# One fixed issue order replaced by another in a fused long-convolution and local-attention kernel

## The chip, the cores and the metric

The kernel runs on one core of one Trainium2 chip, as one program in one launch. The metric is the device time of that core in microseconds (us). The kernel before takes 234.37 us, the median of three runs (234.35 to 235.52).

The core has a matmul engine (PE, whose weight loads the profile lists apart as PEld), a vector engine (DVE), an activation engine (ACT), a general engine (POOL) and a queue engine (SP). Each works through its own instruction list in order, and an instruction that waits holds up all that stand behind it in its list. Matmul results land in PSUM and are copied from there by ACT or DVE.

## The reference

x is A_q, of 2048 rows (positions) and 640 columns, in bfloat16. Two branches read it, and a gate for each row mixes them.

```
g = sigmoid((x * gate_w).sum(-1))
# A: a causal convolution as long as the sequence
k_shift = 4-tap causal filter of A_k along the positions
kv = k_shift * A_v
y  = irfft(rfft(kv, 2S) * rfft(ssm_k, 2S))[:S] + kv * ssm_D
a  = x * y
# B: attention of 32 heads of 20 columns; position s sees s, s-2, ..., s-14
q, k, v = split(x @ wqkv)
b = softmax(q . k / sqrt(20), over the 8 positions) . v  @ wo
out = g * a + (1 - g) * b
```

## The kernel before, in words

**Attention.** x is transposed by PE (`xpose`, L449) into xT. `vproj` (L525) makes v, and `qkproj` (L572) makes q and k transposed, for five column blocks ft, into staging tiles stg. `fragger` (L619 to L622) then moves the rows of each head by DMA from stg to 32-row slots in three sets of tiles, qb and kb, most of them issued from POOL's queue. `score_gen` multiplies qb by kb for four heads at a time (L648), ACT takes the exponential into ETall (L655), `pv_gen` multiplies by v (L679), and DVE divides by the sums (L689, L692). `op_tr` transposes the result, and `outproj` (L879) multiplies it by wo in 32 units of five matmuls. Each unit is copied out by ACT (L884) or DVE (L886) into bl, scaled by 1 - g.

**Convolution.** DVE filters A_k in eight blocks of seven instructions (`conv`, L471 to L486) and multiplies by v (L490). The transform of the 2048 positions is done in two matmul stages, for the filter (`h_stream`) and the data (`u_stream`), each for two halves P of the columns: `s1_unit` (L713, L715) and `s2_unit` (L734). Each unit is copied out of PSUM by ACT (L244) or DVE (L246). The filter's transform is kept twice: in place (H for half 0, SX for half 1) and with its two partition halves swapped (Hw). The swap (`swaps`, L830) goes in four steps of two DMAs per half; between two steps POOL copies one element (L824), so that a step waits until the one before it has landed. `products` (L766) multiplies both forms by the data's transform on DVE, 22 instructions per half. `inverse1` (L845) is the first inverse stage, ten units of 16 matmuls per half, and `final` (L927) the second, in six pieces of two or three groups of rows.

**The end.** `load_q` brings x in again, 1024 rows at a time: q0 for pieces 1 to 3 of `final`, q1 for pieces 4 to 6. Each of the two is four DMAs on SP's queue (L902). The third and fourth are paced: POOL reads one element of the first (second) part out of q into link (L897), so it waits for that part's landing, and clears one element of the next part (L898), which the next DMA waits for. DVE then scales q by g in eight instructions (L905). For each piece, DVE multiplies the piece by q (L939), adds bl (L941), and four DMAs on SP's queue write it out (L944). They wait for L941.

**What sets the order.** The parts are generators that yield requests (an engine or a choice of two, dependencies, PSUM slots). `Steps.run` reads the string ORDER: each letter names a generator, whose pending request is granted and its instructions issued; a `-` ahead of it picks the second of two engines (DVE for a copy out of PSUM). The string therefore fixes each engine's list, the engine of each copy and, because slots are handed out first in, first out, the PSUM slot of each unit. There are four slots of two banks; a small unit takes half of one. Costs, moves and lags that stand in the requests are read by nothing in this program. Waits are put in by the framework wherever one instruction needs another's data or tile. The DMAs of `final` are no requests: they are issued in the same step as L941.

Of the kernel before, what the change touches and what calls it, by code (L numbers as in the profile page):

```python
# [17 lines left out]
S = 2048  # L18
D = 640
# [94 lines left out]

STREAMS = "abcdefghijklmnopqrstuvwxyz0123456789ABCDEFGHIJKLMNOPQRSTUVWXYZ"
ORDER = """
a-aa-aw-wawww-aiw-ia-awwi-ii-iaaiia-aa-aaaw-wi-ii-ii-iifiiiiii-iiifwwcccwwwwcfcccccccccccfffwwwwcwfwwwffccwww-ww-wcccccccccwwwffww
wfdddddccccciccccccccccccccccxff-xfifcidiifficcccfiiddddddccixxiccxciiffdxddefiidfiifeicccccccii-iiiiidddxxxxxffxxxffdfffcccfxxxxx
-xxxi-idddddexedddddii-xfiiiiiiffdddffxlccccxieidddfedcdiii-iddddfiiiy-iyy-yyxiyyxiyy-yyiyx-idddddecfcd-xxed-xccccdccfcccccccccccc
icccciiifdddyiyiecdfffdddediifidiccdcdddifeddcc-iccdfdie-iid-idddfdi-iifyi-yyyyyeiidedidddddx-ixfx-xdyyy-yccccccccy-yyjiyjccccccci  # L120
fccdddddidedddjff-iif-idyj-ydicccccdidddeedddiifefgiidcddddiii-icdeccccdccccgcdjjdddie-ididd-iiiiiddcdgcccclgcccedddeyyycc-yyyycdd
-yccyyy-yccjddeedzddd-zdcccdzc-zzzz-zoddzdd-zzzz-zeddddeddzd-zzdddd-zzoodd-zdeeddddz-zzzz-zddzzzdqde-zdddddozoooooeduzz-zzzoeezzz
-zzz1-111111-1111-1111-111000-0001-1ooo00uu0-000oooooo000-00-00ooo0r0-r10-101r021rr2221-r1r-r00221111r-ru111111ss3ss1313111331ss3u
s333s3333333333p333ss00220020ss0ss2ssss000s002s0000555555555550552252222uvv225vv55522254-5-44-4vvvv4444u4vv-444u444vvvu444puuuuu4
-4tts-stvtststtsssssst-tts-ss-ssss-ssttstttsss-ss-stssttstt-tsts-sttttttsstsstssssttts-ssttst
"""


# [88 lines left out]
def kernel(  # L217
# [21 lines left out]
    def raw(ap, off, dims):  # L239
        return bass.AP(tensor=ap.tensor, offset=ap.offset + off, ap=dims)  # L240
# [27 lines left out]
    G = p0.tile([128, 32, 2, 128], BF, name="G", tag="G")  # L268
# [40 lines left out]
    def ev(name):  # L309
        if name not in E:  # L310
            E[name] = Ev()
        return E[name]

    def mark(name, g, lag=0.0):
        x = ev(name)
        x.src, x.lag = g.done.src, lag
# [48 lines left out]
    def bulk(ft):  # L365
        if ft == 0:
            yield from load_k(1)
            yield from load_k(2)
            g = yield Req("G", 3900.0)
            masks(2)  # L370
            yield from load_corners()
            yield from small()
            yield from load_h(0)
        if ft == 1:
            for a in range(4):
                yield from load_G(a)
                yield from load_v(0, a)
        if ft == 2:
            for a in range(4):
                yield from load_v(1, a)  # L380
        if ft == 3:
            yield from load_h(1)
# [213 lines left out]
    def fragger():  # L596
        left = {}
        for h in range(H):
            for f in range(DH * h // 128, (DH * h + DH - 1) // 128 + 1):
                left[h // 4] = left.get(h // 4, 0) + 2  # L600
        for ft in range(NDT):
            f0 = 128 * ft
            hs = list(range(f0 // DH, (f0 + 127) // DH + 1))
            got = {}
            for h, w in ([(h, w) for h in hs for w in range(2)] if ft == 0 else [(h, w) for w in range(2) for h in hs]):
                if w not in got:
                    yield Req("N", 0.0, [ev(f"pj{ft}{w}")])
                    got[w] = frags.pop(0)
                    assert got[w][:2] == (ft, w)
                _, _, stg, evs, free = got[w]  # L610
                wd = KW if w else QW
                fa, fb = max(DH * h, f0), min(DH * h + DH, f0 + 128)
                t, rows = h // 4, fb - fa
                r0 = 32 * (h % 4) + fa - DH * h
                dst = (ksets if w else qsets)[t % 3]
                deps = list(evs) + ([ev(f"sc{t - 3}")] if t >= 3 else [])
                near = ft == 0 and w == 0
                if near:
                    g = yield Req("S", 450.0, deps, move=20.0 * rows)  # L619
                else:  # L620
                    g = yield Req("G", 510.0, deps, move=20.0 * rows)
                (nc.sync if near else nc.gpsimd).dma_start(dst[r0:r0 + rows, 0:wd], stg[fa - f0:fb - f0, 0:wd])  # L622
                left[t] -= 1
                if near:
                    mark(f"near{t}", g)
                if not left[t]:
                    mark(f"set{t}", g)
                if h == hs[-1]:
                    free.src = g.done.src
            yield from bulk(ft)  # L630
        mark("frags", g)
# [258 lines left out]
    def load_q(half):  # L890
        yield Req("N", 0.0, [ev(f"{k}s2{P}") for k in "hu" for P in range(2)] if half else [ev("hs10"), ev("hs11")])
        q = p0.tile([128, 8, D], BF, name=f"q{half}", tag="G" if half else "HL")
        st[f"q{half}"] = q
        for g in range(4):
            if g > 1:
                x = yield Req("G", 200.0, [r0.done])
                nc.gpsimd.tensor_copy(link[32 * g - 64:32 * g - 32], q[32 * g - 64:32 * g - 32, 0, 0:1])  # L897
                nc.gpsimd.memset(q[32 * g:32 * g + 32, 0, 0:1], 0.0)  # L898
            if g:
                r0 = r  # L900
            r = yield Req("S", 600.0, [x.done] if g > 1 else [], move=1450.0)
            nc.sync.dma_start(q[32 * g:32 * g + 32], raw(x2, (32 * (g // 2) + g % 2 + 16 * half) * D, [[64 * D, 32], [2 * D, 8], [1, D]]))  # L902
        for t in range(8):
            r = yield Req("D", 297.0, [Ev(r.done.src, 2500.0), ev("gate")] if t == 0 else [])
            nc.vector.tensor_scalar(q[:, t], q[:, t], g_nat[:, 8 * half + t:8 * half + t + 1], None, ALU.mult)  # L905
        mark(f"qg{half}", r)

# [40 lines left out]
    for gen in (xpose, h0_slot, fragger, score_gen, pv_gen, conv, conv_v, conv_end, qkproj, gate, x_slot, h_slot, p2_slot,  # L948
                u_slot, swaps, load_T, load_wo, op_tr, outproj, final):
        plan.add(gen(), gen.__name__)  # L950
    for gen in (load_q, vproj, h_stream, u_stream, products, inverse1):
        for P in range(2):
            plan.add(gen(P), f"{gen.__name__}{P}")
# [31 lines left out]
```

## Time and profile before

| | |
|---|---|
| three runs | 234.35, 234.37, 235.52 us |
| the profiled execution, a fourth | 235.92 us, with a span of 233.9 us from first to last instruction |
| granted PE clock over the span | 0.966 of full |
| matmuls / weight loads / DVE / ACT / POOL instructions | 3537 / 3537 / 272 / 250 / 137 |
| moved by DMA | 33.86 MB, mean 145 GB/s |

Busy time is what the profile counts while an engine runs an instruction. A queue name with a q behind it (SPq, POOLq) is the engine's sequencer, which waits for semaphores and issues DMAs. In a timeline row stand the start, the length, the engine and line, the operation with tiles and shapes, and in brackets the idle time before it with what ended it. In a row of stretches stand, for each engine, the busy time and the number of instructions, then the granted PE clock as a share of full speed.

### The profile page before, as it was taken

How to read it: one execution, taken by the hardware profiler on the slowest of the kernel's cores; microseconds unless marked ns; L12 is line 12 of the kernel's file. 1: busy time of each engine (PE TensorE's matmuls, PEld its weight loads, DVE VectorE, ACT ScalarE, POOL GpSimd, SP SyncE). 2: the span in 40 equal slices, each digit the busy share in tenths (PEclk: the TensorE clock that was granted, in tenths of full speed). 3: DMA queues.
4: the chain of work that ended last, by engine and by line, in shares of the span. 5: the costliest groups of instructions: out<-in, count | busy, mean ns of one | idle time of the engine just before them, and what ended most of it. 6: DMA issues, size and time to landing. Idle time of an engine off the chain costs nothing.

```text
span 233.9 us, 8338 instructions
## 1 busy us (share of the span) xinstructions
PE 213.4 (91%) x3537; PEld 172.5 (74%) x3537; DVE 190.7 (82%) x272; ACT 173.0 (74%) x250; POOL 60.1 (26%) x137
## 2 busy tenths in 40 slices
PE   7999999788999999999998898999999599889890
PEld 3886987567767767767676587988887499889770
DVE  4655997995877898789999877999659996967971
ACT  0343659436989999898999878997999396765480
POOL 6900780443061622712350000000000390000000
PEclk9999999979999999999999859999999799999998
DMA  6999599699999999879747675474590509003545
GB/s 208 354 196 295 145 184 173 130 137 141 177 186 197 199 151 152 147 125 123 114 98 195 172 169 116 109 175 115 119 196 7 112 3 205 3 3 87 124 116 131
DMA packets 69560, 33.86 MB, mean 145 GB/s; under 512 B 51476, under 2 KB 67220, under 8 KB 69524
## 3 DMA queue, kind: packets, MB, share of 16 engines
q1 hardware_dynamic: 66356, 28.35, 62.7%
q0 software_dynamic: 2880, 4.90, 9.8%
q8 instruction: 27, 0.44, 0.8%
q10 hardware_dynamic: 288, 0.09, 0.2%
q14 instruction: 9, 0.07, 0.1%
HBM read 20.04 MB, written 2.62 MB: 97 GB/s over the span
## 4 chain that ended last, share of the span: by engine, by line
PE 52%; DVE 17%; DMA 14%; issue 6%; POOL 4%; ACT 3%; SPq 1%; DVEq 0%; POOLq 0%
PE PS L572 15%; PE PS L879 6%; DMA Hw<-SX 6%; PE PS L679 5%; PE PS L845 5%; PE PS L648 5%; DVE SX L246 4%; PE PS L525 4%; PE PS L734 3%; DMA kb<-stg 3%; DVE SX L766 3%; DVE Hw L766 3%; DMA q<-in_A_q_dram 2%; PE PS L927 2%; DMA KX<-in_A_k_dram 2%
## 5 line engine op out<-in xcount | busy, mean ns | idle before, releaser
L655 ACT ACTIVATE ETall<-PS 121x912 bf16<-121x912 f32 (+1 forms) x80 | 64.7, 867 | 6.5 <-PE PS L648 6.2
L572 PE MATMUL PS<-xT,Wqk 128*128 128x342 bf16 (+1 forms) x300 | 50.5, 313 | 2.3 <-DVE VW L692 2.0
L244 ACT CAST UC<-PS 128x1024 bf16<-128x1024 f32 (+2 forms) x47 | 43.6, 1053 | 8.4 <-PE PS L845 4.9
L572 PEld LDWEIGHTS <-Wqk 128*128 128x128 bf16 x300 | 27.8, 98 | 17.3 <-issue 2.9
L471 DVE TENSOR_TENSOR KX<-KX 128x1280 bf16<-128x1280 bf16 x32 | 27.8, 894 | 1.9 <-DMA KX<-in_A_k_dram 1.5
L525 PE MATMUL PS<-WvT,xT 128*121 128x320 bf16 x180 | 27.8, 305 | 0.0
L622 POOL DMA_DIRECT2D qb<-stg x29 | 14.6, 505 | 44.5 <-ACT stg L244 26.0
L244 ACT CAST stg<-PS 128x342 bf16<-128x342 f32 (+1 forms) x38 | 17.0, 467 | 11.3 <-PE PS L572 9.4
L525 PEld LDWEIGHTS <-xT 128*121 128x121 bf16 x180 | 23.8, 137 | 1.3 <-issue 0.2
L879 PE MATMUL PS<-wo,oT 128*128 128x320 bf16 x160 | 24.2, 302 | 0.1
L622 POOL DMA_DIRECT2D kb<-stg x36 | 18.0, 510 | 21.6 <-ACT stg L244 15.6
L734 PEld LDWEIGHTS <-G 64*128 64x128 bf16 x512 | 19.1, 96 | 4.7 <-issue 3.7
L879 PEld LDWEIGHTS <-oT 128*128 128x128 bf16 x160 | 21.2, 145 | 1.3 <-issue 0.2
L648 PE MATMUL PS<-qb,kb 31*128 31x114 bf16 x576 | 20.5, 218 | 1.4 <-DMA kb<-stg 0.9
L648 PEld LDWEIGHTS <-kb 31*128 31x128 bf16 x576 | 12.5, 96 | 10.5 <-issue 7.9
L845 PE MATMUL PS<-F,Hw 128*128 128x128 bf16 x160 | 19.4, 227 | 0.1
L246 DVE CAST UC<-PS 128x1024 bf16<-128x1024 f32 (+1 forms) x15 | 17.6, 1215 | 2.2 <-ACT UC L244 1.8
L679 PEld LDWEIGHTS <-ETall 121*128 121x128 bf16 x576 | 17.6, 97 | 1.7 <-issue 0.3
L679 PE MATMUL PS<-VW,ETall 121*128 121x63 bf16 (+2 forms) x576 | 18.6, 186 | 0.0
L845 PEld LDWEIGHTS <-Hw 128*128 128x128 bf16 x160 | 18.3, 117 | 0.3 <-DVE Hw L766 0.3
L244 ACT CAST VW<-PS 121x320 bf16<-121x320 f32 x26 | 11.2, 432 | 9.5 <-PE PS L525 9.5
L246 DVE CAST stg<-PS 128x363 bf16<-128x363 f32 (+1 forms) x22 | 11.5, 527 | 7.8 <-PE PS L572 6.1
(80 smaller groups left out, 353.0 us busy)
## 6 DMA issues: line engine op xcount, KB each, us to landing
xn<-in_A_q_dram SPq DMA_DIRECT2D x8, 320.0 KB
h_lin<-in_A_ssm_k_dram SPq DMA_DIRECT2D x16, 160.0 KB
vin<-in_A_v_dram SPq DMA_DIRECT2D x8, 320.0 KB
Hw<-H SPq DMA_DIRECT2D x8, 320.0 KB
q<-in_A_q_dram SPq DMA_DIRECT2D x8, 320.0 KB
Hw<-SX SPq DMA_DIRECT2D x8, 320.0 KB
kb<-stg POOLq DMA_DIRECT2D x28, 85.1 KB, 4.1
G<-cf_G SPq DMA_DIRECT2D x4, 512.0 KB
```

The costliest lines, as they stand in the source:

```text
L244: nc.scalar.copy(dst, src)
L246: nc.vector.tensor_copy(dst, src)
L471: eng.tensor_tensor(d, kin[:, n + 3 - j:n + 3 - j + m, :], w.to_broadcast([128, m, QC]), ALU.mult)
L525: nc.tensor.matmul(ps[0:BK, 0:320], lhsT=xT[:, dt, s0:s0 + BK], rhs=Wv[:, dt, 320 * hp:320 * hp + 320], start=(dt == 0), stop=(dt == NDT - 1))
L572: nc.tensor.matmul(ps[:, 0:n], lhsT=Wqk[:, dt, w, 128 * ft:128 * ft + 128], rhs=xT[:, dt, s0:s0 + n], start=(dt == 0), stop=(dt == NDT - 1))
L622: (nc.sync if near else nc.gpsimd).dma_start(dst[r0:r0 + rows, 0:wd], stg[fa - f0:fb - f0, 0:wd])
L648: nc.tensor.matmul(sc[:, hh, BQ * bb:BQ * bb + BQ], lhsT=kb[r:r + DH + NF, BK * b:BK * b + 128], rhs=qb[r:r + DH + NF, BQ * b:BQ * b + BQ] ...
L655: nc.scalar.activation(ETall[0:BK, e, :, 0:BQ * nb], sc[0:BK, :, 0:BQ * nb], ACT.Exp, scale=SCALE)
L679: nc.tensor.matmul(O[:, (b - b0) // 6, c0:c0 + 21 * nh], lhsT=ETall[0:BK, e, hh, BQ * bb:BQ * bb + 128], rhs=VW[0:BK, b, 4 * t + h4:4 * t ...
L734: nc.tensor.matmul(ps[:, c, 160 * jj:160 * jj + 160], lhsT=G[rows, j0 + jj, rr, :], rhs=Am[rows, rr].rearrange("p o (q j) l -> p j (o q) l ...
L845: nc.tensor.matmul(d, lhsT=st[(key, P)][:, c, o + il // 4, :, il % 4], rhs=M[:, k, :], start=(k == 0), stop=(k == 1), skip_group_check=True)
L879: nc.tensor.matmul(op, lhsT=oT[:, ft].rearrange("p h m a -> p a (h m)")[:, t, :], rhs=wo[:, ft, 320 * n:320 * n + 320], start=(ft == 0), s ...
```

## The change

Nothing is computed otherwise. ORDER is replaced whole, by a string with the same letters the same number of times, and five numbers in requests are changed: the move of a head row from 20 to 28 ns, lags of 800 and 500 ns behind the marks near and set, and the lag between the last load of q and its first scaling from 2500 to 4500 ns. As nothing in the program reads these five, the instructions differ by ORDER alone.

```diff
 ORDER = """
-a-aa-aw-wawww-aiw-ia-awwi-ii-iaaiia-aa-aaaw-wi-ii-ii-iifiiiiii-iiifwwcccwwwwcfcccccccccccfffwwwwcwfwwwffccwww-ww-wcccccccccwwwffww
...
+a-aaw-wwaa-ww-awwwwwa-aia-a-ii-iia-a-iiia-ai-iaaiii-ii-iiiiiffiiiwi-ww-wfwwfffwwwww-ww-wwwwwfffwww-ww-wfffccccccccwwccciccii-iiii
...
 """
...
-                    g = yield Req("S", 450.0, deps, move=20.0 * rows)
+                    g = yield Req("S", 450.0, deps, move=28.0 * rows)
...
-                    g = yield Req("G", 510.0, deps, move=20.0 * rows)
+                    g = yield Req("G", 510.0, deps, move=28.0 * rows)
...
-                    mark(f"near{t}", g)
+                    mark(f"near{t}", g, 800.0)
...
-                    mark(f"set{t}", g)
+                    mark(f"set{t}", g, 500.0)
...
-            r = yield Req("D", 297.0, [Ev(r.done.src, 2500.0), ev("gate")] if t == 0 else [])
+            r = yield Req("D", 297.0, [Ev(r.done.src, 4500.0), ev("gate")] if t == 0 else [])
```

SP's list from the swap of half 1 to the first output, before (SX to Hw is the swap, L902 loads q, L325 loads the tables T into SX and wo, L944 writes the output):

```order
L830 DMA Hw_2309<-SX_2075 64x5x512 x2
L902 DMA q0_2466<-in_A_q_dram 32x8x640
L830 DMA Hw_2309<-SX_2075 64x5x512 x6
L902 DMA q0_2466<-in_A_q_dram 32x8x640
L325 DMA SX_2075<-cf_T 128x4x512
L902 DMA q0_2466<-in_A_q_dram 32x8x640
L902 DMA q1_3479<-in_A_q_dram 32x8x640 x4
L325 DMA SX_2075<-cf_T 128x4x512
L944 DMA out_0_dram<-q0_2466 32x3x640 x8
```

The same stretch of SP's list in the changed kernel:

```order
L830 DMA Hw_2288<-SX_1942 64x5x512 x4
L325 DMA SX_1942<-cf_T 128x4x512
L325 DMA wo_2289<-in_B_wo_dram 128x5x640
L830 DMA Hw_2288<-SX_1942 64x5x512 x2
L325 DMA SX_1942<-cf_T 128x4x512
L902 DMA q0_2460<-in_A_q_dram 32x8x640 x2
L830 DMA Hw_2288<-SX_1942 64x5x512 x2
L902 DMA q0_2460<-in_A_q_dram 32x8x640 x2
L944 DMA out_0_dram<-q0_2460 32x3x640 x4
L902 DMA q1_3369<-in_A_q_dram 32x8x640 x4
L944 DMA out_0_dram<-q0_2460 32x3x640 x4
```

The four loads of q1 moved from ahead of all output to behind the output of the first piece; the loads of T and wo and the first two of q0 moved in between the steps of the swap.

DVE's list at the end of the products and in the first piece of `final`, before (L766 products, L246 copies of the inverse into UC and of `final` into yb, L905 scaling of q, L886 `outproj` into bl):

```order
L766 TENSOR_TENSOR H0_287<-UC_2755,H0_287 128x80x8
L766 TENSOR_TENSOR Hw_2308<-UC_2755,Hw_2308 128x80x8
L246 CAST UC_2755<-PS_63 128x128x8 x3
L905 TENSOR_SCALAR q1_3479<-q1_3479,g_nat_68 128x640 x2
L905 TENSOR_SCALAR q0_2466<-q0_2466,g_nat_68 128x640
L905 TENSOR_SCALAR q1_3479<-q1_3479,g_nat_68 128x640 x2
L246 CAST UC_2755<-PS_63 128x128x8
L905 TENSOR_SCALAR q0_2466<-q0_2466,g_nat_68 128x640
L905 TENSOR_SCALAR q1_3479<-q1_3479,g_nat_68 128x640 x3
L905 TENSOR_SCALAR q0_2466<-q0_2466,g_nat_68 128x640 x6
L246 CAST UC_2755<-PS_63 128x128x8
L886 TENSOR_SCALAR bl_3112<-PS_63,omg_69 128x320
```

In the changed kernel, from the last two products to the first copy out of the inverse:

```order
L766 TENSOR_TENSOR SX_1942<-UC_2737,SX_1942 128x80x8
L766 TENSOR_TENSOR Hw_2288<-UC_2737,Hw_2288 128x80x8
L905 TENSOR_SCALAR q0_2460<-q0_2460,g_nat_68 128x640
L886 TENSOR_SCALAR bl_3105<-PS_63,omg_69 128x320
L905 TENSOR_SCALAR q0_2460<-q0_2460,g_nat_68 128x640 x2
L246 CAST UC_2737<-PS_63 128x128x8 x2
```

And further down, around the first piece of `final`:

```order
L246 CAST yb2_3557<-PS_63 128x2x3x160
L939 TENSOR_TENSOR q0_2460<-yb2_3557,q0_2460 128x1920
L886 TENSOR_SCALAR bl_3105<-PS_63,omg_69 128x320
L941 TENSOR_TENSOR q0_2460<-q0_2460,bl_3105 128x1920
L905 TENSOR_SCALAR q1_3369<-q1_3369,g_nat_68 128x640 x2
L886 TENSOR_SCALAR bl_3105<-PS_63,omg_69 128x320
L905 TENSOR_SCALAR q1_3369<-q1_3369,g_nat_68 128x640 x5
L939 TENSOR_TENSOR q0_2460<-yb2_3557,q0_2460 128x1920
```

Before, the products of half 1 (SX) come first and those of half 0 (H) last; now half 0 comes first. The scaling of q0 stands right behind the products, ahead of the copies out of the inverse, and the scaling of q1 stands between the first and the second piece of `final`, ahead of a copy out of `outproj`.

Further up, seven copies out of PSUM move from ACT to DVE up to the end of the filter's transform: two of the filter's half 1, one of its half 0, three net of `qkproj` and one net of `vproj`. DVE runs the third and fourth filter blocks and the start of the fifth, 16 instructions, without a copy in between; before, it was nine.

More of the change, by code (lines that the diff above doesn't have):

```diff
@@ L116 @@
 ORDER = """
-a-aa-aw-wawww-aiw-ia-awwi-ii-iaaiia-aa-aaaw-wi-ii-ii-iifiiiiii-iiifwwcccwwwwcfcccccccccccfffwwwwcwfwwwffccwww-ww-wcccccccccwwwffww
[L118 to L125, printed above, removed]
+a-aaw-wwaa-ww-awwwwwa-aia-a-ii-iia-a-iiia-ai-iaaiii-ii-iiiiiffiiiwi-ww-wfwwfffwwwww-ww-wwwwwfffwww-ww-wfffccccccccwwccciccii-iiii
+-iddddddiiifxx-iddddciiiiiiiiddddiiiieddddddccccfccxxxccfffffxffffffxcccccfffffcccxxxxxxxxxxxicfccccexxccccccfcccccccccccccccccccc
+ccccciiiccddddddiedddcccfcf-iife-iidffffiiidddddicifedxddedidd-x-iiddiddffieddddcddcc-iiel-ii-iddcidyf-yyfycccyx-xfycccccccccccccc
+ccciiiy-yyyyeyddie-iiiyyy-yyii-yyyddi-ididccccdeffdddcccc-idddid-ieifiididddfdxdiidfefid-x-ifdddxxxxxfxexccxxccccccxjdyyffeiccccce
+fjcc-iiiiiiiijf-icdddddgiiicdccccc-idi-iddy-yddiddddeg-igidjidddidiiideddjgedeyyy-yddy-yyyyddjdcccccccc-yydd-ydjycccccccyy-yyyecdl
+dddezddd-zdccccz-zzczzcccccddd-zdzccdcc-zdeeddzdddo-zdz-zzdde-zddddzooded-zddz-zddddeeodzdd-zzdd-zdoooz-zzd-zdeddddedzdzz-zzzeezzz
+-zzz0ozz-0001-100ooo0-0000-0oo00000-001o0-1111-1o1o1111-11000-10o0-000022222p11110r-rrrqr0-rr0211200-rr-r002001-1111oo221ss2ssp220
+02222202uu2s022ossoo33s11111sss1s3333333ssss3113331uu1111u1u33444433443s4s44334433444u444444s-ssu55u5-55-5555555uuuu-s55u555-555tt
+tsssss-tt-sststvvvvvvvvs-svvvvvttssttsssssssvtsttt-ttssssssssst-sttt-tttttttsstsstsssttsstt-stsst
 """
```

## The prediction

> **What bounds the kernel now.** I read the page's head first, then the busy time by stretches, then the chain of work that ended last, then the timeline at the places where the chain leaves PE.
>
> ```profile
> span 233.9 us, 8338 instructions
> PE 213.4 (91%) x3537; PEld 172.5 (74%) x3537; DVE 190.7 (82%) x272; ACT 173.0 (74%) x250; POOL 60.1 (26%) x137
> PE 52%; DVE 17%; DMA 14%; issue 6%; POOL 4%; ACT 3%; SPq 1%; DVEq 0%; POOLq 0%
> ```
>
> ```profile
> 24.00:65.00 41.00, 38.03 (x424) 29.98 (x422) 35.39 (x49) 27.35 (x53) 17.34 (x50) 0.96 0.99 154
> 65.00:147.00 82.00, 78.92 (x1523) 58.39 (x1520) 71.07 (x101) 74.77 (x104) 23.80 (x61) 0.96 0.84 152
> 147.00:184.00 37.00, 32.93 (x476) 29.21 (x474) 32.40 (x43) 33.91 (x44) 0.84 (x5) 1.00 0.55 126
> 184.00:205.00 21.00, 19.69 (x320) 19.35 (x320) 19.16 (x37) 14.72 (x16) 7.81 (x4) 0.92 0.32 69
> ```
>
> After the length of a stretch stand the busy times of PE, PEld, DVE, ACT and POOL. PE is nearly always busy, but from 65 to 147 ACT and DVE are close behind (74.77 and 71.07 of 82 us): the front is a balance of three. From 147 on the chain shows one place where PE stands:
>
> ```profile
> 147.85 0.59 SPq L830
> 165.65 0.62 SPq L830
> 172.07 0.66 DVE SX L766
> 183.95 0.41 DVE Hw L766
> 184.40 12.27 PE PS L845 x191
> ```
>
> The swap of SX takes from 147.85 to about 172, the 22 products of half 1 take 12.3 us (172.07 to 184.35), and only then can the first inverse start. PE has run out of other work:
>
> ```profile
> 184.00 0.29 PE L845 MATMUL PS<-F,SX 128*128 128x128 bf16 x1 [3.06 <-DVE SX L766]
> 184.00:186.00 2.00, 1.89 (x17) 1.71 (x18) 2.00 (x5) 0.00 (x0) 1.06 (x1) 0.50 0.61 106
> 186.00:187.60 1.60, 1.60 (x19) 1.60 (x18) 1.60 (x4) 1.01 (x1) 1.60 (x1) 0.56 0.04 10
> 187.60:190.00 2.40, 2.40 (x47) 2.40 (x45) 2.40 (x6) 2.20 (x3) 2.40 (x1) 1.00 0.00 0
> ```
>
> The idle costs 3.06 us, and the granted clock then stands at about half for 3.6 us, which is another 1.8 us of PE's time. The tail runs from the first piece's L941 to the last:
>
> ```profile
> 209.39 1.16 DVE L941 TENSOR_TENSOR q<-q,bl 128x1920 bf16<-128x1920 bf16 x1
> 210.58 1.76 SPq L944 DMA_DIRECT2D out_dram<-q  x4
> 228.39 0.82 DVE q L941
> ```
>
> 210.55 to 229.21 is 18.66 us, and 4.7 us follow for the last output.
>
> **Part 1: the front, to 147.** Up to there seven copies leave ACT for DVE:
>
> ```profile
> L244 ACT CAST stg<-PS 128x342 bf16<-128x342 f32 (+1 forms) x38 | 17.0, 467 | 11.3 <-PE PS L572 9.4 <-issue 1.1 <-DMA KX<-in_A_k_dram 0.5
> L246 DVE CAST SX<-PS 128x1024 bf16<-128x1024 f32 (+1 forms) x13 | 15.2, 1195 | 2.6 <-PE PS L734 1.5 <-PE PS L713 0.5 <-ACT ETall L655 0.5
> L244 ACT CAST H<-PS 128x1024 bf16<-128x1024 f32 (+1 forms) x12 | 11.6, 1004 | 0.5 <-PE PS L734 0.2
> ```
>
> With 1.0 us for each of the three large ones and 0.45 for each of the four small ones ACT loses 4.8 us; DVE at 1.2 and 0.5 us gains 5.6. If ACT paces the front alone, 4.8 us come off; if DVE does, 5.6 come on. With 74.77 and 71.07 the two trade places at nearly the same sum. The longer run of filter instructions on DVE could make PE wait for copies that stand behind it; the record has one wait of PE for DVE, 2.02 us, with a slow clock after it:
>
> ```profile
> 47.43 1.62 PE L572 MATMUL PS<-xT,Wqk 128*128 128x349 bf16 x5 [2.02 <-DVE VW L692]
> 47.40:50.00 2.60, 2.57 (x20) 1.33 (x20) 2.57 (x5) 0.89 (x2) 0.26 (x1) 0.51 1.13 132
> ```
>
> The changed order may lose this wait and gain others behind seven more filter instructions. I take **0** for the front, ends -4.8 and +5.6.
>
> **Part 2: half 0 first.** The products of half 0 need a swap that lies a stage earlier, and the swap of SX is covered by them. Between 147 and 181 ACT is busy nearly throughout (33.91 us in the row to 184), and its share falls by about one copy, so PE comes to the first inverse at about the same time, and the 3.06 us and the 1.8 us of slow clock go: **-4.8**. At least -3.1 (the slow clock stays), at most -6 (that one copy too). Two units of `outproj` that stood ahead of the inverse now stand behind it; PE does them either way.
>
> [...]
>
> **Part 3: the scaling of q0.** q0's third and fourth loads wait for POOL's copies L897. A record of such a copy beside products:
>
> ```profile
> 180.98 0.82 SPq L902 DMA_DIRECT2D q<-in_A_q_dram  x2
> 184.94 7.43 POOL L897 COPY link<-q 32x1 bf16<-32x1 bf16 x1 [19.55 <-DMA q<-in_A_q_dram]
> 192.54 0.81 SPq L902 DMA_DIRECT2D q<-in_A_q_dram  x2
> 192.57 0.19 POOL L897 COPY link<-q 32x1 bf16<-32x1 bf16 x1
> ...
> L905 DVE TENSOR_SCALAR q<-q,g_nat 128x640 bf16<-128x640 bf16 x16 | 5.0, 386 | 0.0
> L886 DVE TENSOR_SCALAR bl<-PS,omg 128x320 bf16<-128x320 f32 x8 | 4.3, 548 | 3.3 <-PE PS L879 3.2
> ```
>
> The first load landed 3.96 us after its issue. The copy, 0.19 us when nothing disturbs it, then took 7.43 us, while DVE ran 14 products one behind the other, and ended at 192.37, when a product had to wait for ACT. In the changed kernel the first two loads of q0 are issued after the third step of the swap of SX, behind T, at some 160 us, and land near 170. From about 169 to 189 DVE runs products of both halves in one row (14 of half 0 are left, 22 of half 1, at 12.28 / 22 = 0.56 us each: 20 us). So the copies come through at about the end of the products. Then: 0.2 us for the copy, 0.2 to the issue, 0.4 to the second issue, 3.96 to land, 4.8 us, and the whole of it on DVE, because the scaling stands right behind the products. In its shadow PE starts inverse 1, whose 2nd and 3rd units are copied by DVE; with four slots it does four units of 16 matmuls (47 matmuls in 2.40 us above: 3.3 us), then waits until DVE has scaled three rows and copied (5.0 / 16 = 0.31 three times, 0.55 and 1.2: 2.7 us). PE stands 4.8 + 2.7 - 3.3 = 4.2 us, and the slow clock behind it costs up to 1.8. I take **+5**, ends 0 and +5.7. If instead POOL's copy for the swap's last step is the one caught (L824, 0.19 us undisturbed), the last step is issued at 177 and lands 5.4 us later (147.85 to the copy below), DVE waits that long ahead of half 1, in which time q0's copies pass: +5.4, the same size.
>
> ```profile
> 153.25 0.19 POOL L824 COPY Hw<-Hw 128x1 bf16<-128x1 bf16 x1 [11.44 <-DMA Hw<-SX]
> ```
>
> **Part 4: q1 behind the first output.** This is the largest term. SP issues the first output when L941 has ended and q1's loads behind it. From L941's end: four outputs 1.76; first load to landing 3.96; POOL's copy and clear and the issue of the third 0.4; the issue of the fourth 0.4; its landing 3.96: **10.5 us** in which DVE stands at q1's first scaling. The ends: 9.4, if a landing takes 3.4 as the quickest 32 KB move to qb does, and 13.4, if it takes 5.43, since in the record q1's last load was issued at 192.94 and used at 198.37:
>
> ```profile
> 192.54 0.81 SPq L902 DMA_DIRECT2D q<-in_A_q_dram  x2
> qb<-stg POOLq DMA_DIRECT2D x1, 32.1 KB, 3.4
> 198.37 1.56 DVE q L905 x5
> ...
> 205.30 1.02 PE PS L927 x96
> 206.32 3.55 PE PS L879 x25
> ```
>
> Behind it in DVE's list stands a copy of `outproj` (L886). Its half slot is wanted again by PE three units later, so PE goes on for 5.3 us after the first piece (six units of `outproj` at 3.55 / 5 = 0.71, one piece at 1.02), while L941 ends 4.2 us after it (206.32 to 210.55), then stands. What is left afterwards on DVE:
>
> ```profile
> L939 DVE TENSOR_TENSOR q<-yb,q 128x1920 bf16<-128x1920 bf16 (+1 forms) x6 | 6.3, 1042 | 1.1 <-ACT yb L244 1.0
> L941 DVE TENSOR_TENSOR q<-q,bl 128x1920 bf16<-128x1920 bf16 (+1 forms) x6 | 6.3, 1047 | 0.3
> L246 DVE CAST yb<-PS 128x960 bf16<-128x960 f32 x2 | 2.3, 1158 | 0.4 <-PE PS L927 0.3
> ```
>
> 8 scalings at 5.0 / 16 = 0.31, 3 L886 at 0.55, 5 L939 and 5 L941 at 1.05, and two copies of pieces, 2.3: 16.9 us. PE has 15 units and four pieces, some 14.5 us, so DVE is the bound, with about 0.5 us of waits. 10.5 + 17.4 - 18.66 = **+9.2**; ends +8 and +12.
>
> **Sum.** 0 - 4.8 + 5 + 9.2 = +9.4 us. The profiled execution took 235.92 us (span 233.9 and 2.0 around it) and would take 245.3; it lies 1.55 above the median of the runs, so the median goes from 234.37 to **243.8**.
>
> **Rivals.**
> *The copies slip through.* If q0's first loads land before the row of products begins, or a product waits for ACT in time, Part 3 is 0: 234.37 - 4.8 + 9.2 = 238.8. For it: 169 and 170 lie close together. Against it: the record above, 14 products without a gap. [...]
>
> *The filter run starves PE.* If the front's +4 to +5 comes on top: about 248.
>
> *Faster: ACT paces the front.* The copies taken from it let the exponentials close up. ACT idles 7.2 us between 65 and 147; if all of that and the 4.8 went, the front would be 12 us shorter: 231.8. It decides from 10.6 us on. Against it: DVE needs 71.07 + most of 5.6 of the 82 us, so at most some 6 us can come out before DVE is full; only if DVE started with a lead would more.
>
> *The change does nothing here or there.* The five durations alone do nothing; the order acts everywhere.
>
> **How the numbers follow.** The main case (243.8) has 0.58, its own range 240 to 247.5 from the ends of Parts 1 to 4 without adding them all. Slipping through has 0.20 (238.8), a starved front 0.11 (248), the shorter front 0.07 (231.8), and a front 8 to 10 us shorter, which would end within 0.5% of before, 0.04. The range 237 to 249 leaves out the last two and the ends of the others. 0.5% (1.2 us) is about what three runs of this kernel can tell from no change. Slower: 0.58 + 0.20 + 0.11 = 0.89; same 0.04; faster 0.07.
>
> **What would show it.** Part 4: in the timeline SP issues four outputs, then two loads of q; DVE is idle some 10 us ahead of a scaling of q, ended by a DMA, and PE some 10 us in `outproj` (L879). If that idle is under 3 us, Part 4 is wrong. Part 3: a copy L897 or L824 on POOL of several us, and DVE idle of about 5 us ahead of L905 or the products of SX. Part 2: no idle of PE ahead of the first inverse matmul. Part 1: the last exponential starts where it does before, within the ends given:
>
> ```profile
> 143.69 0.75 ACT L655 ACTIVATE ETall<-PS 121x684 bf16<-121x684 f32 x1
> ```
>
> The prediction as a whole fails if the front gains more than 6 us.

## The result and the profile after

The changed kernel takes 254.66 us, the median of four runs (252.60 to 255.16), against 234.36 for the kernel before (four runs, 234.00 to 235.52): a ratio of 1.084, 95% interval 1.077 to 1.091, and 20.3 us. The forecast was 243.8 with a range of 237 to 249. The sign and the places were right, the size was not: the loss is about twice as large. Medians here and below are over all runs of a kernel; a ratio and its interval leave out slow runs, those some 1.5% above the quickest of the same kernel.

The head of the page of the changed kernel, its busy times and the shares of its chain of work that ended last:

```profile
span 252.9 us, 8353 instructions
PE 216.4 (86%) x3537; PEld 172.7 (68%) x3537; DVE 194.5 (77%) x277; ACT 170.4 (67%) x245; POOL 68.9 (27%) x137
PE 34%; DMA 19%; DVE 13%; issue 11%; POOL 11%; ACT 6%; SPq 3%; POOLq 0%; DVEq 0%; ACTq 0%
```

DMA, POOL and "issue" have grown, and PE's busy time with them by 3 us. From the chain itself (start, length, what), the places that carry this:

```profile
149.23 0.59 SPq L830
...
174.39 15.77 POOL link L897
...
190.74 5.99 DMA q<-in_A_q_dram
196.81 0.06 DVE q L905
...
197.71 9.89 PE PS L845 x128
...
208.69 1.06 PE PS L927 x96
...
213.82 0.33 SPq L944
...
216.11 5.39 DMA q<-in_A_q_dram
...
221.96 4.31 DMA q<-in_A_q_dram
226.35 0.68 DVE q L905 x2
...
227.55 4.28 PE PS L879 x20
...
236.07 1.48 PE PS L927 x153
237.55 2.17 issue
...
247.78 0.82 DVE q L941
```

Both waits of DVE that the forecast named are there: POOL's copy L897 took 15.77 us among the products, so q0 landed late, and q1's loads were issued behind the first output. The two waits, and what PE did behind them, from the timeline (in brackets the idle time of the engine and what ended it):

```profile
196.81 0.39 DVE L905 TENSOR_SCALAR q<-q,g_nat 128x640 bf16<-128x640 bf16 x1 [6.71 <-DMA q<-in_A_q_dram]
197.71 0.27 PE L845 MATMUL PS<-F,SX 128*128 128x128 bf16 x1 [5.10 <-DVE bl L886]
226.35 0.68 DVE L905 TENSOR_SCALAR q<-q,g_nat 128x640 bf16<-128x640 bf16 x2 [12.56 <-DMA q<-in_A_q_dram]
227.55 4.28 PE L879 MATMUL PS<-wo,oT 128*128 128x320 bf16 x20 [12.51 <-DVE bl L886]
239.72 0.55 PE L927 MATMUL PS<-UC,SX 32*32 32x160 bf16 x39 [2.17 <-issue]
```

The stretches at a slow clock (after the length the busy times of PE, PEld, DVE, ACT and POOL, then the granted clock):

```profile
197.70:203.00 5.30, 5.29 (x51) 5.29 (x51) 4.84 (x10) 1.01 (x1) 0.00 (x0) 0.50 0.00 0
227.50:230.50 3.00, 2.95 (x12) 1.86 (x12) 3.00 (x8) 0.61 (x2) 0.00 (x0) 0.51 0.00 0
240.90:244.00 3.10, 3.10 (x13) 1.99 (x12) 1.74 (x2) 2.17 (x4) 0.00 (x0) 0.50 0.47 108
```

Each of PE's three stands (5.10, 12.51 and 2.17 us) is followed by three to five microseconds at half clock.

The two profiled executions (235.92 and 255.16 us, spans 233.9 and 252.9) differ by 19.0 us in the span. By four marks it comes together so. The first is the start of the last exponential, which in the changed kernel stands in the timeline:

```profile
144.20 0.75 ACT L655 ACTIVATE ETall<-PS 121x684 bf16<-121x684 f32 x1
```

| from, to | before, us | after, us | difference |
|---|---|---|---|
| start to the last exponential (143.69, 144.20) | 143.69 | 144.20 | +0.5 |
| to the first matmul of the first piece (205.30, 208.69) | 61.61 | 64.49 | +2.9 |
| to the end of its L941 (210.55, 213.79) | 5.25 | 5.10 | -0.2 |
| to the end of the last L941 (229.21, 248.60) | 18.66 | 34.81 | +16.2 |
| to the end of the span | 4.69 | 4.30 | -0.4 |

Two of these stretches come back in the experiments, each read from the profile of the kernel in question: the middle one (last exponential to the first piece) and the tail (end of the first L941 to the end of the last).

### The profile page after: what moved, and what is told of

Read it like the earlier page. It is cut to its first block, busy times and chain, and to the rows that moved or that the text cites. A ratio compares the mean times of both kernels' runs of the same rounds, so it can differ in the third digit from the quotient of the medians.

```text
span 252.9 us, 8353 instructions
## 1 busy us (share of the span) xinstructions
PE 216.4 (86%) x3537; PEld 172.7 (68%) x3537; DVE 194.5 (77%) x277; ACT 170.4 (67%) x245; POOL 68.9 (27%) x137
## 4 chain that ended last, share of the span: by engine, by line
PE 34%; DMA 19%; DVE 13%; issue 11%; POOL 11%; ACT 6%; SPq 3%; POOLq 0%; DVEq 0%; ACTq 0%
PE PS L572 9%; DMA Hw<-SX 7%; POOL link L897 6%; DMA q<-in_A_q_dram 6%; PE PS L879 5%; PE PS L845 4%; DMA kb<-stg 4%; ACT ETall L655 3%; PE PS L679 3%; POOL qb L622 3%; PE PS L525 2%; POOL kb L622 2%; DMA h_lin<-in_A_ssm_k_dram 2%; PE PS L449 2%; DVE SX L246 2%
## 5 line engine op out<-in xcount | busy, mean ns | idle before, releaser
L879 PE MATMUL PS<-wo,oT 128*128 128x320 bf16 x160 | 27.1, 327 | 12.5 <-DVE bl L886 12.5
L525 PE MATMUL PS<-WvT,xT 128*121 128x320 bf16 x180 | 26.4, 300 | 0.9 <-ACT ETall L655 0.7
L622 POOL DMA_DIRECT2D qb<-stg x29 | 14.5, 504 | 45.6 <-ACT stg L244 22.8
L897 POOL COPY link<-q 32x1 bf16<-32x1 bf16 x4 | 16.3, 4078 | 35.3 <-DMA q<-in_A_q_dram 35.3
L244 ACT CAST stg<-PS 128x342 bf16<-128x342 f32 (+1 forms) x35 | 15.6, 471 | 14.6 <-PE PS L572 12.8
L884 ACT ACTIVATE bl<-PS,omg 128x320 bf16<-128x320 f32 x26 | 13.8, 563 | 16.8 <-PE PS L879 16.6
L648 PEld LDWEIGHTS <-kb 31*128 31x128 bf16 x576 | 13.4, 95 | 12.5 <-issue 10.2
L845 PE MATMUL PS<-F,Hw 128*128 128x128 bf16 x160 | 20.9, 234 | 0.0
L734 PEld LDWEIGHTS <-G 64*128 64x128 bf16 x512 | 17.9, 93 | 4.2 <-issue 2.2
L905 DVE TENSOR_SCALAR q<-q,g_nat 128x640 bf16<-128x640 bf16 x16 | 5.3, 380 | 19.3 <-DMA q<-in_A_q_dram 19.3
L246 DVE CAST UC<-PS 128x1024 bf16<-128x1024 f32 (+1 forms) x14 | 16.4, 1209 | 4.6 <-PE PS L845 4.3
L246 DVE CAST stg<-PS 128x363 bf16<-128x363 f32 (+1 forms) x25 | 13.0, 522 | 8.5 <-PE PS L572 8.5
```

Of the source, the lines that this page charges most:

```text
L244: nc.scalar.copy(dst, src)
L246: nc.vector.tensor_copy(dst, src)
L525: nc.tensor.matmul(ps[0:BK, 0:320], lhsT=xT[:, dt, s0:s0 + BK], rhs=Wv[:, dt, 320 * hp:320 * hp + 320], start=(dt == 0), stop=(dt == NDT - 1))
L648: nc.tensor.matmul(sc[:, hh, BQ * bb:BQ * bb + BQ], lhsT=kb[r:r + DH + NF, BK * b:BK * b + 128], rhs=qb[r:r + DH + NF, BQ * b:BQ * b + BQ] ...
L734: nc.tensor.matmul(ps[:, c, 160 * jj:160 * jj + 160], lhsT=G[rows, j0 + jj, rr, :], rhs=Am[rows, rr].rearrange("p o (q j) l -> p j (o q) l ...
L845: nc.tensor.matmul(d, lhsT=st[(key, P)][:, c, o + il // 4, :, il % 4], rhs=M[:, k, :], start=(k == 0), stop=(k == 1), skip_group_check=True)
```

## The experiments

Times scatter by some 1% from one set of runs to the next, so each kernel stands beside the median of the kernel before in its own set. Where an interval is given, it is the 95% interval of the ratio to that kernel. In line numbers, those behind an insertion in the products are shifted by two or six; this is said where such a row is shown.

**q1's loads ahead of the first output.** v is `load_q` of q1, u that of q0, t `final`, s `outproj`.

```diff
-...3113331uu1111u1u334...
+...3113331uu1111u1uvvvvvv334...
-...tttsssss-tt-sststvvvvvvvvs-svvvvvtts...
+...tttsssss-tt-sststvvs-svvvvvtts...
```

> The changed kernel with the four loads of q1, and POOL's two copies between them, issued right behind the last load of q0; the scalings of q1 stay where they are in DVE's list. Theory (the loads stand in SP's list behind an output that waits for L941): the 12.56 us of DVE ahead of q1's scaling and the 12.5 us of PE go, and with them the half clock behind; from the first L941's end to the last one's end some 18 to 20 us in place of 34.8; 238 to 240 us. Rival (the landing or the scalings themselves hold DVE): over 248 us.

241.08 us against 235.61, a little above the 238 to 240 of the theory; three of the four runs lie at 240.97 to 241.37, one at 237.17. The changed kernel is 20.3 us above before, this one 5.5: by the medians the place of six requests is worth 14.8 us. The tail is now 20.70 us (214.01 to 234.71) in place of 34.81, 14.1 less; DVE doesn't wait for q1, and PE stands nowhere in `outproj`. The copy of Part 3 is caught in this profile as in that of the changed kernel (first row), so the two compare. One thing remained, which no theory had named:

```profile
173.63 16.85 POOL L897 COPY link<-q 32x1 bf16<-32x1 bf16 x1 [4.03 <-DMA q<-in_A_q_dram]
222.23 1.48 PE PS L927 x153
223.71 2.11 issue
225.82 0.55 PE PS L927 x39
```

The 2.1 us inside the fifth piece are there without any wait for q1.

**The same move made in the kernel before.** Loads and scalings of q1 behind the first piece; the fourteen v further up in the string are taken out there (not shown):

```diff
-...s-stvtststts...
+...s-sttststtvvvvvvvvvvvvvvs...
```

> The kernel before with the loads of q1 and its eight scalings moved behind the output of the first piece of final, all else in its place. Theory (Part 4 is a price of this one move): DVE idle 10 to 13 us ahead of q1's scaling, PE idle about as long, slow clock behind it; +11 to +15 us on before. By the prediction's own term +9.2. Rival (the loss in the changed kernel needs its other moves): under +4.

250.50 us (249.68 to 251.76) against 235.06, ratio 1.069 (1.062 to 1.076): 15.4 us between the medians, just above the 11 to 15 of the theory; the tail is 35.37 us (207.57 to 242.94), 16.7 more than before, as in the changed kernel and not the +9.2 of the forecast. Against that the middle stretch is 59.96 us (142.36 to 202.32), 1.7 less: q1's scalings no longer hold up DVE ahead of the last copies of the inverse. One edit in the other order gives the whole loss of Part 4:

```profile
219.92 2.46 DVE L905 TENSOR_SCALAR q<-q,g_nat 128x640 bf16<-128x640 bf16 x8 [12.35 <-DMA q<-in_A_q_dram]
223.50 0.96 PE L879 MATMUL PS<-wo,oT 128*128 128x320 bf16 x3 [14.14 <-DVE yb L246]
```

**q1's loads left late, its scalings moved back.** Eight D requests of v go to just ahead of the fourth piece's L939 (one of them comes from a place that is not shown):

```diff
-...ststvvvvvvvvs-svvvvvtts...
+...ststvvvvvvs-stts...
-...t-sttt-tttttt...
+...t-sttt-tvvvvvvvvttttt...
```

> The changed kernel with the eight scalings of q1 moved in DVE's list to right ahead of the fourth piece's product by q, which is the first to use them; the loads stay behind the first output. Theory (DVE's order holds PE, through the copy of outproj behind the scaling): the second and third piece pass while the loads travel, PE's idle of 12.5 us shrinks to a few us, 242 to 246 us. Rival (with the loads behind the output the end is bound by their landing anyway): 252 us or more.

241.95 us (236.81 to 243.91) against 235.61, 14.0 us less than the changed kernel. The tail is 23.45 us (207.10 to 230.54) in place of 34.81, 11.4 less. The loss of Part 4 shrinks although the loads are where they were: DVE's list held PE, not the landing as such. The wait for q1 that is left:

```profile
221.38 2.46 DVE L905 TENSOR_SCALAR q<-q,g_nat 128x640 bf16<-128x640 bf16 x8 [3.81 <-DMA q<-in_A_q_dram]
```

This profiled execution, the quickest of its four, shows something else too. POOL's copy came through after 2.38 us, at the moment at which DVE had to wait 0.40 us for the last step of the swap, and PE did not stand ahead of the second inverse:

```profile
175.46 2.38 POOL L897 COPY link<-q 32x1 bf16<-32x1 bf16 x1 [5.29 <-DMA q<-in_A_q_dram]
178.19 0.66 DVE L766 TENSOR_TENSOR SX<-UC,SX 128x960 bf16<-128x960 bf16 x1 [0.40 <-DMA Hw<-SX]
```

So the rival "the copies slip through" is here another execution of lists that are the same up to the products: the swap's last step landed after the last product of half 0, and DVE had to wait for it. In the profiled run of the changed kernel it had landed before, and the copy stayed shut out to the end of the products. How often the one and the other come, these profiles don't tell.

**q0 without POOL's copies.** The two u of these requests are taken out of ORDER as well:

```diff
-            if g > 1:
+            if g > 1 and half:
                 x = yield Req("G", 200.0, [r0.done])
...
-            r = yield Req("S", 600.0, [x.done] if g > 1 else [], move=1450.0)
+            r = yield Req("S", 600.0, [x.done] if g > 1 and half else [], move=1450.0)
```

> The changed kernel with the third and fourth load of q0 issued without POOL's copy and clear ahead of them; q1 stays paced. Theory (POOL's copy is shut out by the products, 15.78 us, and delays q0): PE's 5.10 us ahead of the first inverse of half 1 and most of its slow clock (2.6 us) go, 247 to 248 us. Rival (the products or the slots hold PE there, q0 only happens to be late too): 253 us or more.

250.27 us (247.22 to 254.03) against 235.61, ratio 1.059 (1.050 to 1.067). The median lies 2 us above the 247 to 248 of the theory and 3 below the rival's. The profiled execution, at 254.03, was the longest of the four, and there the copy caught was the other one, which paces the swap's last step:

```profile
170.75 7.55 POOL L824 COPY Hw<-Hw 128x1 bf16<-128x1 bf16 x1 [9.65 <-DMA Hw<-SX]
183.83 0.66 DVE L766 TENSOR_TENSOR SX<-UC,SX 128x960 bf16<-128x960 bf16 x1 [5.58 <-DMA Hw<-SX]
```

It came through at the end of half 0's products; the last step landed late, and DVE stood 5.58 us ahead of half 1. PE stood 4.38 us ahead of the second inverse, for this reason now. With the one copy gone the other takes its turn.

**Both edits.** 

> The changed kernel with both of these edits. If Parts 3 and 4 are the whole loss and add up, the gain of Part 2 is left: 254.7 - 16 - 7.5 = 231 us, range 229 to 234. Rival (the front or the products of half 0 cost something as well): above 235 us.

233.26 us (ten runs, 232.05 to 237.12) against 235.61, ratio 0.991 (0.987 to 0.994). The two take back the loss and 2.3 us more, within the range that was expected; the estimate from adding them up, 231, which is 3.4 us below the 234.36 of its time, was a little too good. In the profile no wait of DVE or PE is left at the two places. The middle stretch is 56.71 us (144.84 to 201.55), 4.9 less than in the profile of before. Against that, the last exponential starts 1.2 us later, and the tail is 20.89 us (206.65 to 227.55), 2.2 more, with the same wait in it again:

```profile
218.66 0.55 PE L927 MATMUL PS<-UC,SX 32*32 32x160 bf16 x39 [2.31 <-issue]
```

**Which instruction lets POOL in.** Three small DVE instructions among the products of half 1, behind the 6th, the 12th and the 18th:

```diff
                 nc.vector.tensor_tensor(X, U, X, ALU.mult)
+                if P == 1 and key == "w" and k == 2:
+                    nc.vector.memset(wgz[:, 0, 0:16], 0.0)
+                if P == 1 and key == "w" and k == 5:
+                    nc.vector.tensor_copy(wgz[:].rearrange("p a b -> p (a b)"), Dz[:])
+                if P == 1 and key == "w" and k == 8:
+                    nc.vector.tensor_scalar(wgz[:], wgz[:], omg[:, 0:1], None, ALU.mult)
```

> The changed kernel with three more, small DVE instructions among the 22 products of half 1, whose results nothing uses: a memset of 16 columns behind the 6th, a copy of 160 columns (one SBUF input) behind the 12th, a multiplication by a scalar of 160 columns behind the 18th. Theory (POOL's copy gets its turn only where DVE waits for a semaphore): the copy caught among the products ends where the products end, about 190, as in the changed kernel. Rivals (any instruction with fewer than two SBUF inputs lets POOL in): it ends behind the memset, near 181.4, or behind the copy, near 185, or behind the scaling, near 188.5. If no copy of POOL is caught in this execution, it tells nothing.

My theory fell. The caught copy (here L903) ended with the memset, not with the products:

```profile
177.06 7.28 POOL L903 COPY link<-q 32x1 bf16<-32x1 bf16 x1 [4.61 <-PE PS L734]
184.25 0.07 DVE L768 MEMSET wgz<- 128x8 uint32 x1
```

In the second probe the copy stands behind the 6th product, the multiplication by a scalar behind the 12th, the memset behind the 18th.

> The changed kernel with three small DVE instructions among the products of half 1, in another order than in lock_probe: the copy of 160 columns (one SBUF input) behind the 6th product, the multiplication by a scalar behind the 12th, the memset behind the 18th. If any instruction with fewer than two SBUF inputs lets POOL in, its caught copy ends behind the 6th product, 3.5 us after the first product of half 1; if only one without SBUF inputs does, behind the 18th, some 10 us after it.

```profile
172.89 11.46 POOL L903 COPY link<-q 32x1 bf16<-32x1 bf16 x1 [3.98 <-DMA q<-in_A_q_dram]
180.71 0.20 DVE L768 COPY wgz<-Dz 128x160 bf16<-128x160 bf16 x1
184.23 0.26 DVE L770 TENSOR_SCALAR wgz<-wgz,omg 128x160 bf16<-128x160 bf16 x1
184.59 3.36 POOL L903 COPY link<-q 32x1 bf16<-32x1 bf16 x1
187.85 0.07 DVE L772 MEMSET wgz<- 128x8 uint32 x1
```

The bf16 copy at 180.71, with one SBUF input, let nobody in; the multiplication at 184.23 freed the first POOL copy (172.89 + 11.46 = 184.35), the memset at 187.85 the second (184.59 + 3.36 = 187.95). So neither rival holds as it was written: the number of SBUF inputs does not decide it alone. Why the multiplication freed POOL and the bf16 copy did not is open.

**Memsets in the changed kernel.** A memset behind every fourth product, in both halves, and nothing else:

```diff
                 nc.vector.tensor_tensor(X, U, X, ALU.mult)
+                if key == "w" and k % 2 == 0:
+                    nc.vector.memset(wgz[:, 0, 0:16], 0.0)
```

> The changed kernel with a DVE memset of 16 columns (0.07 us each, results unused) behind every fourth product, twelve in all; nothing else is moved. Theory after the probe (an instruction without SBUF inputs lets POOL's waiting copy in): no copy of POOL is caught for more than 3 us, PE does not stand ahead of the first inverse of half 1, Part 3 is gone and Part 4 stays: 246 to 248 us. Rival (the probe's execution slipped through by chance): 252 us or more.

247.90 us (246.21 to 248.87) against 235.73, ratio 1.053 (1.044 to 1.062): 12.2 us above before, where the changed kernel is 20.3 above. PE does not stand ahead of the inverse, and the middle stretch is 56.68 us (143.43 to 200.11) in place of 64.49. Part 3 costs about 8 us. POOL's copies (L899 here) pass:

```profile
173.47 0.68 POOL L899 COPY link<-q 32x1 bf16<-32x1 bf16 x1 [4.36 <-DMA q<-in_A_q_dram]
174.69 0.60 POOL L899 COPY link<-q 32x1 bf16<-32x1 bf16 x1 [0.39 <-DMA q<-in_A_q_dram]
```

**The fourth and the fifth piece apart.** On top of both edits, two units of `outproj` between these pieces:

```diff
-...-sttt-tttttttsstsstsss...
+...-sttt-tttssssttttttsss...
```

> The kernel with both edits (q1 early, q0 unpaced) and, further, two units of outproj moved between the fourth and the fifth piece of final, which in the changed kernel stand one behind the other in PE's list. Theory (384 small instructions in 2 us outrun the fetch of PE's instructions, which takes 1.3 us beside the output): PE's 2.3 us of idle inside the fifth piece shrinks to under 1 us and its half clock goes; 1.5 to 3 us less than with both edits alone, 230 to 231.5 us. Rival (PE waits for something else there, a slot or a copy): no change, 233.

232.44 us (six runs, 230.78 to 238.75) against 235.06, ratio 0.990 (0.983 to 0.996). The median is 0.8 us below that of both edits in another set, inside the scatter, and above the 230 to 231.5 of the theory. The profiles tell more. The wait itself shrank from 2.31 to 0.61 us (the next two kernels, which keep the pieces apart, have 0.36 and 1.01), the granted clock behind it stays at 1.00 in all three, where that of both edits stands at 0.50 for two microseconds and more, and the tail is 18.82, 18.58 and 19.24 us, where both edits have 20.89 and q1 early alone 20.70. So the pieces apart are worth some 1.5 to 2.3 us in the traces. The wait, and POOL's copy in the same execution:

```profile
225.71 0.64 PE L927 MATMUL PS<-UC,SX 32*32 32x160 bf16 x49 [0.61 <-issue]
172.63 6.82 POOL L824 COPY Hw<-Hw 128x1 bf16<-128x1 bf16 x1 [10.38 <-DMA Hw<-SX]
```

This execution, 238.75, is the longest of its six, and the second row goes with that: again the copy ahead of the swap's last step was caught, and PE stood 4.58 us ahead of the inverse of half 1.

**The last step of the swap without POOL's copy.**

```diff
-                    if last is not None:
+                    if last is not None and not (P and c and o):
                         x = yield Req("G", 150.0, [last.done])
```

> The same, and the last step of the swap of SX issued without POOL's copy ahead of it, so that no product can hold it back. Theory (in some executions that copy is the one caught, as in q0_unpaced, where it took 7.55 us and DVE stood 5.58): the median changes little, the executions some 4 us above the others vanish; 230 to 231.5 us. Rival (the fourth step collides with the third and both land late): 1 to 3 us more.

232.17 us (twelve runs, 230.52 to 235.78) against 235.06, ratio 0.992 (0.987 to 0.997). The median is unchanged, as expected, though above the 230 to 231.5 that was named; two of the twelve runs still lie at 235.30 and 235.78, without a profile of either, so this tells little.

**Memsets on top of both edits and the pieces apart.** 

> The kernel with q1 early, q0 unpaced and the fourth and fifth piece apart, with the same twelve memsets. Theory: the executions in which a copy of POOL is caught (238.75 of that kernel) vanish, the quick ones stay: 230 to 232 us, no execution above 234. Rival (the slow executions have another cause, on the chip): the same spread as without.

231.16 us (six runs, 229.96 to 232.49) against 235.73, ratio 0.983 (0.978 to 0.989). No run is above 232.5, and POOL's copies among the products take at most 0.64 us in the profile. Since only one run of six was long in `apart`, six runs without one do not prove the cause. This is the quickest of the kernels, 1.7% below before.

**Half 0 first in the kernel before.** Places keep their engine and kind of work; the numbers of the halves are dealt out anew (0 and 1 the transform of the data, 2 and 3 the products, 4 and 5 the inverse).

```diff
-...0-r10-101r021rr2221-r1r-r00221111r-ru111111ss3ss1313111331ss3us333s3333333333p333ss00220020...
+...0-r00-000r020rr2220-r0r-r00220000r-ru000000ss2ss1212111221ss2us222s2222222333p333ss11331131...
```

> The kernel before with half 0 first from the second stage of the data's transform on: each place of the order keeps its kind of work and its engine, but the first eleven units, the first 22 products and the first ten inverse units are those of half 0, the rest those of half 1. Theory (Part 2: the swap of SX is covered by the products of half 0): PE's 3.06 us ahead of the first inverse and its slow clock go, 3 to 5 us less than before, ratio 0.979 to 0.988. Rivals: the wait only moves (PE stands ahead of the inverse of half 1 or in the transform instead), within 1 us of before; or a copy of POOL is caught by the longer row of products and the loads of q come late, slower than before.

233.18 us (six runs, 230.66 to 234.07) against 236.53, ratio 0.989 (0.980 to 0.998). PE is busy all through the beginning of the inverse; one wait ahead of `final`, 1.50 before, grew:

```profile
176.00:190.00 14.00, 13.97 (x245) 13.13 (x243) 12.60 (x23) 14.00 (x19) 4.19 (x4) 1.00 0.29 55
200.96 1.02 PE L927 MATMUL PS<-UC,SX 32*32 32x160 bf16 x96 [2.23 <-DVE UC L246]
201.98 5.23 PE PS L879 x25
202.00:206.00 4.00, 4.00 (x18) 2.67 (x19) 2.78 (x4) 2.57 (x4) 0.00 (x0) 0.57 0.01 4
```

The middle stretch is 58.34 us (142.62 to 200.96) in place of 61.61: -3.3. About half of it is lost again at once: behind the longer wait the clock stands at 0.57, the same 25 matmuls of `outproj` that took 3.55 us in the kernel before take 5.23, and the tail grows by 1.6. So the wait moved in part, as the first rival had it. The ratio is just above the range that was expected of it.

## Why the prediction was right in the places and wrong in the size

**Part 1, the front: within its ends.** +0.5 us in the profiled pair against 0. In the eleven profiled executions with this front the last exponential starts between 143.39 and 147.17, with a median of 144.20, and in the three with the front before at 142.36, 142.62 and 143.69. So the new front is likelier a loss of one or two microseconds, which is also a part of what both edits fell short of 231. It was not tried by itself.

**Part 2, half 0 first: right in kind, too high by itself.** The gain was forecast at -4.8. PE does not stand ahead of the first inverse in the changed kernel. Its middle stretch grew by 2.9 us, of which Part 3 accounts for 7.75 (below), which leaves -4.9; the profiles of both edits and of the memsets, in which no copy holds up q0, give -4.9 directly (56.71 and 56.68 against 61.61). That this meets the -4.8 is luck. Put alone into the kernel before, half 0 first gave -3.3, with 0.7 us of longer wait ahead of `final` in it. The rest fits something that the forecast did not count: q1's scalings no longer stand ahead of the last copies of the inverse on DVE, which by itself, in the kernel before with q1 late, gave -1.7 in this stretch (59.96 against 61.61).

**Part 3, the scaling of q0: right in mechanism, +7.75 where +5 was taken.** The copy came through at the end of the products, as forecast. From there every step was longer: the last load needed 5.99 us (3.96 taken), DVE stood 6.71 (4.8), PE 5.10 (4.2), and the half clock behind it lasted 5.3 us, which costs 2.65 (up to 1.8). One step was different: PE was let go by the copy of `outproj` (L886) 0.9 us after DVE went on, not after three scalings and a copy of the inverse (2.7 us), and it had run only 2.5 us beyond the products, not 3.3: 6.71 + 0.9 - 2.5 = 5.1. The cost is near 8 us by the memsets as well: 64.49 - 56.68 = 7.8. The forecast gave the copy being caught and its slipping through a chance each, as if one of them were the kernel's. Profiles show both for the same lists: caught in the changed kernel and with q1 early (16.85 us), let through after 2.38 us with q1's scalings moved back. The four runs of the changed kernel, 252.60 to 255.16, show no run that is some 8 us quicker.

**Part 4, q1 behind the first output: right in the wait, and the term that failed, +16.2 where +9.2 was taken.** It holds 7.0 of the 10.9 us that lie between 243.8 and 254.66. Two steps failed.

The wait itself was 12.56 us, not 10.5. The sum stood on landings of 3.96 us; here the chain has 5.39 us for the first pair of loads, which travel beside the first output, and 4.31 for the last. The end that the text gave, 13.4, was nearer than the middle.

The larger part is the step "PE has 15 units and four pieces, some 14.5 us, so DVE is the bound, with about 0.5 us of waits". From 226.35 to 248.60 there were 22.25 us, not 17.4. PE was the bound. Its work, without slow clock and waits, is some 14.2 us (227.55 to 247.02, less 2.17 of waiting and 3.1 lost to the clock), as reckoned; it was slower than that by what the forecast left out: half clock for 3.0 us after its long stand (1.5 us lost), then 2.17 us of "issue" inside the fifth piece, then half clock again for 3.1 us (1.6 lost): 5.3 us, about the 4.85 by which the stretch is longer. Parts 2 and 3 of the forecast charged the slow clock behind a stand of PE; Part 4, with the longest stand of all, did not.

The 2.17 us were nowhere in the forecast. In the changed order the fourth and the fifth piece stand one behind the other on PE, 192 matmuls and as many weight loads in some 2 us. One queue of the profile, q8 (instruction), moves packets of 16 KB; its 27 packets are 442 KB or some 62 bytes for each of the 7,074 matmuls and weight loads. It moved none from 217 to 236.9, while PE mostly stood, and one from 237.04 to 238.38, 1.34 us, in which the outputs travel too; PE went on at 239.72, 1.34 us behind its end. In every one of the fourteen profiled executions PE has such a wait inside the fifth piece and goes on 1.2 to 1.6 us behind the end of a packet of q8. That PE waits for its own instructions is inferred from this and from `apart`, in which 1.6 us of other work between the two pieces took 1.7 us off the wait. The kernel before has the same wait once, with 0.51 us, 1.42 us behind a packet that ended at 220.60.

The rest of the sum holds: the runs' +20.3 are the 19.0 of the two profiled spans, and 1.3 by which the executions shown lie differently to their medians (235.92 to 234.36, 255.16 to 254.66) and around their spans. The rivals "starved front" and "shorter front" did not happen.

## What to carry to other kernels

After a stand of PE, charge the slow clock behind it in every term (here 3.0 to 5.3 us at 0.50 or 0.51 behind stands of 2.17 to 12.51 us), and where work piles up behind a wait, ask again which engine is the bound at that clock. A load that is issued from a queue behind an output inherits the output's wait, and an in-order list that has its consumer early passes the wait on to engines that do not need the data: here moving the loads took 14.1 us off the tail, and moving the consumer 11.4. Small instructions of GpSimd that pace DMAs should not stand beside long rows of two-input products; here a memset of 0.07 us behind every fourth product let them pass and took about 8 us off.

## What was not expected of the hardware

- POOL's 32-element copy was shut out for 15.78 us across 28 back-to-back DVE products with two SBUF inputs, without a turn between them. A DVE memset of 0.07 us or a wait of DVE of 0.40 us ended it; a bf16 copy of 160 columns on DVE did not.
- PE stood inside two adjacent pieces of small matmuls, for nothing but "issue", in all eight profiled executions that have them adjacent in PE's list: 2.1 to 2.6 us in seven, 3.95 in the kernel with q1's scalings moved back. With ten matmuls of `outproj` between them it was 0.4 to 1.0 us.
- Clock: 5.10 us of idle cost 5.3 us of half clock, 12.51 us only 3.0, and 2.17 us of idle 3.1; the length of the slow stretch did not follow the length of the stand. Behind the third stand the clock fell only some 1 us after PE went on at 239.72 (0.84 over 240 to 241, 0.50 over 241 to 242). The fall came behind a stand of 2.17 us here, as it came behind one of 2.02 us in the profile of before (0.51 from 47.40 to 50.00).
